# One core of a state-space mixer block: a smaller last transform, a new parameter table, and low weight parts kept in DRAM

## The chip, the core and the metric

The kernel runs on one core of a Trainium2 chip. The metric is the device time of one execution in microseconds (us), the median of several runs. A profiled execution gives a trace of every engine: PE (matrix multiply, with PEld for its weight loads), DVE (vector), ACT (activation functions and copies), POOL (general purpose, here mostly issuing transfers) and SP (issuing transfers only). Transfers issued by SP, ACT and POOL run on 16 shared DMA engines.

## The reference

With L = 2048 tokens and D = 576 channels, `_A_ref` is a state-space convolution along the tokens and `_B_ref` a two-layer network over the channels with F = 4608 hidden units:

```python
dt = jnp.exp(log_dt)
A = -jnp.exp(log_A_real) + 1j * A_imag
C = (C_real + 1j * C_imag) * dt[:, None]
P = jnp.exp((A * dt[:, None])[:, :, None] * pos[None, None, :])
K = 2.0 * jnp.einsum("dn,dnl->dl", C, P).real
y = irfft(rfft(u_t, 2 * L) * rfft(K, 2 * L))[:, :, :L]
s = y + u * D_skip
...
x = A_u
xn = _layernorm(x, axis=-1)
s = _A_ref(xn, ...)
g = _silu(_B_ref(xn, ...))      # layernorm, gelu(y @ w1 + b1) @ w2 + b2
return x + s * g
```

All data is 32-bit floating point.

## The kernel before

Two computations share the core.

**The network.** Tokens go in two halves of 1024, each half in two blocks of 512 (`tb`). The hidden units go in 12 groups of 384 (`g`). A slot is one group for one block, so there are 48 slots: 0 to 23 for the first half of the tokens, 24 to 47 for the second, and two neighbouring slots share a group's weights. To keep precision every operand is split into a high and a low part, and each product is three matmuls (high by high, low by high, high by low). In a slot, `layer1` (L511) makes three hidden tiles with 14 matmuls each, of which the ninth to twelfth and the last read the weights' low parts (`w1l`, `w1s`), and `layer2` (L568) makes eight pieces with 72 matmuls, every third of which reads `w2l`. `split_raw` makes the two parts: SP loads a piece of the weights into `raw` (L451 to L456), ACT rounds it to the high part (L491), DVE subtracts to get the low part (L488). Both halves of the tokens do this for the same 12 groups, so each weight is loaded and split twice. There is one buffer for each of `w1h`, `w1l`, `w2h`, `w2l`, so a group's parts are written after the last matmul of the group before has read its own: layer 1's while layer 2 of the odd slot runs, and layer 2's while layer 1 of the next slot runs.

**The convolution.** Channels go in six chunks of 96. Signal and kernel are cut into two halves of 1024 samples, and each is transformed in two steps. `forward` (L958) does 32-point transforms for both halves, a transpose on DVE (L945) follows, and `s2` (L996) does the 64-point step with the matrix `f2t`. DVE multiplies spectra: `prod` and `sums` (L1012 to L1020) form for the first output half x0 k0, and for the second x0 k1 + x1 k0, where the index names the half of the signal x and of the kernel k. `inverse` (L1042) does the 64-point step back with `g2t`, `back` (L1053) transposes, and `i1` (L1068) does the last 32-point step with `g1t`. In `i1` each matmul contracts over 128 rows, which are the real and imaginary parts of both halves, into 64 outputs: the second half of the output adds what runs over the end of the first half's linear convolution, taken from the imaginary parts with a sign (`odd_rows`). ACT copies the result out and POOL stores it with two transfers (L1077).

The convolution's kernel K itself is made on the chip. `params` computes for each channel and state its decay, angle, phase and size, and `pack` writes a table of 30 numbers for each of them: phase and angle, and powers of the decay with exponents 0 to 7, 0 to 24 in steps of 8 (also with 1024 added), 0 to 224 in steps of 32, and 0 to 768 in steps of 256. Each power is one ACT instruction over 144 channels (L764), the table goes to DRAM in four parts (L773). `tables` reads it back in 36 blocks of 16 channels (L786, on POOL), builds sines and magnitudes on ACT and DVE (L804 to L846), and `kgen` (L885) sums over the states on PE.

**The order.** Every engine's order is written by a planner, the class `Order`, which simulates the engines with estimated durations while it emits the instructions. Work of the network is placed first; steps of other lines (convolution, parameters, tables) are put in where an engine is estimated to be free. `pace` spreads the chunks over the kernel up to an estimated 1060 us. Each engine executes in this fixed order, and an instruction that waits holds up everything behind it on its engine. This holds also for transfers issued on POOL or SP. Towards the end the lines `combine` and `finish` form x + s g and store it.

Of the kernel before, what the change touches and what calls it, by code (L numbers as in the profile page):

```python
# [9 lines left out]
F32 = mybir.dt.float32  # L10
# [22 lines left out]
PK = 144  # L33
NXC, NROW = 1, 4
G = 3
# [18 lines left out]
class Order:  # L54
# [155 lines left out]
def mixer_kernel(ctx, tc, u, log_a_real, a_imag, c_real, c_imag, log_dt, d_skip, w1, b1, w2, b2,  # L210
# [40 lines left out]
    g1t = sb.tile([P, 2, 32], F32, name="g1t")  # L251
# [10 lines left out]
    def load_consts(g):  # L262
        r = slice(32 * g, 32 * g + 32)
        nc.gpsimd.dma_start(f1t[r], f1[r].rearrange("p (k m) -> p k m", k=8)[:, g::4, :])
        h, ri = divmod(g, 2)
        for k in range(h, 2):
            same = k == h
            part = ri if same else 1 - ri
            nc.gpsimd.dma_start(g1t[r, k], g1[64 * part:64 * part + 32, :32])
# [3 lines left out]
    def odd_rows():  # L273
        nc.vector.tensor_scalar(g1t[:32, 1], g1t[:32, 1], -1.0, None, op0=OP.mult)
# [28 lines left out]

    def scale_tv():
        nc.vector.tensor_scalar(tv[:, :32], tv[:, :32], -1.0, MID, op0=OP.mult, op1=OP.add)
        nc.vector.tensor_scalar(tv[:, 32:], tv[:, 32:], 32.0, MID, op0=OP.mult, op1=OP.add)
# [5 lines left out]
    nc.vector.memset(g1t[64:, 0], 0.0)  # L312
# [3 lines left out]
    acc = sb.tile([P, 8, D], F32, name="acc")  # L316


    A2 = sb.tile([P, 16, 2, CH, 2], F32, name="A2")
    A2F = A2.rearrange("p a b c r -> p (a b c r)")  # L320

    PT0 = 3 * D
# [22 lines left out]
    MV, SECOND, PAIR, M4 = {}, [], {}, []  # L345

    def norms(b0, n):
# [3 lines left out]
        def stats(t, part=None):  # L351
# [4 lines left out]
            elif t == 0:  # L356
                a, r = M4 if b0 == 4 else [sb.tile([P, 8], F32, name=m, bufs=2) for m in ("mv", "rs")]
# [107 lines left out]

    def split_raw(low_on=nc.vector):
# [4 lines left out]
        if which == 1:  # L471
            if i == 0 and k:
                w1_tiles()
# [7 lines left out]
        else:  # L481
            if i == 0:
                W[2] = (sb.tile([P, G, D], F32R, name="w2h"), sb.tile([P, G, D], F32R, name="w2l"))
# [3 lines left out]
        def low():  # L487
            low_on.tensor_sub(lo, r[:m], h[:m].bitcast(F32))  # L488
# [178 lines left out]
    def params():  # L667
# [8 lines left out]
        dt = sb.tile([P, 2, SB, 32], F32, name="U").rearrange("p a b c -> p (a b c)")[:, :D]  # L676
# [69 lines left out]
        early.append(step("DVE", d, lambda: V.tensor_mul(nrm, nrm, dt), need=["nrm"]))  # L746

        pt = A2F[:, PT0:PT0 + PK * NPAR].rearrange("p (d k) -> p d k", d=PK)
        ex = [(E1 + k, k) for k in range(1, 8)] + [(E8 + k, HALF * (k // 4) + 8 * (k % 4)) for k in range(1, 8)]
        ex += [(E32 + k, 32 * k) for k in range(1, 8)] + [(E256 + k, 256 * k) for k in range(1, 4)]  # L750

        def pack(i):
            s = slice(i * PK, (i + 1) * PK)

            def columns():
                if i == 0:
                    V.memset(pt[:, :, E1:E1 + 17:8], 1.0)
                V.tensor_copy(pt[:, :, 0], th[:, s])
                V.tensor_copy(pt[:, :, 1], ph[:, s])
                V.tensor_copy(pt[:, :, E256], cr[:, s])  # L760

            def powers(p):
                for k, m in ex[6 * p:6 * p + 6]:
                    A.activation(pt[:, :, k], nrm[:, s], AF.Exp, scale=-float(m))  # L764

            def rest():
                V.tensor_mul(pt[:, :, E256 + 1:], pt[:, :, E256 + 1:], bc(cr[:, s], 2, 3))
            for p in range(4):
                early.append(step("ACT", 1.85, lambda p=p: powers(p), tbl="exp", late=0.0,
                                  need=() if i else [("xn", b) for b in range(4, 8)]))  # L770
            early.append(step("DVE", 0.6 if i else 1.1, columns, need=["polar"]))
            early.append(step("DVE", 0.65, rest))
            early.append(step("POOL", 0.8, lambda: nc.gpsimd.dma_start(par_s[:, s, :], pt)))  # L773
            early.append(step(None, 8.0, lambda: None, mark=("pack", i)))
        for i in range(D // PK):
            pack(i)
        return out, early
# [17 lines left out]
    def tables(b):  # L795
# [36 lines left out]
        def weigh(k, part):  # L832

            if k == 0 and part == 0:
# [4 lines left out]
            if part == 0:  # L839
                nc.vector.tensor_mul(T["U"][:, k], w[:, k, :, 32:], m[:, :, 64:])  # L840
            elif part == 1:
                nc.vector.tensor_mul(v[:, k, :, :32], w[:, k, :, :32], m[:, :, :32])
            elif k == 0:
                nc.vector.tensor_mul(v[:, k, :, 32:], w[:, k, :, 31::-1], m[:, :, 32:64])
            else:
# [14 lines left out]
                + [step("DVE", dve(n), f(weigh, k, part), need=[("sin", b, k)] + ([("kg", b - 1)] if b else []),  # L860
                        mark=("wu", b, k) if part == 2 else None) for k in range(2) for part in range(3)])
# [53 lines left out]
    X1, S2, INV, I1, KG = 1.1, 1.75, 2.15, 3.05, 1.03  # L915

    def chunk(c):
# [24 lines left out]
        def spread(i, x):  # L942
            for g in range(4):
                c0 = 24 * g + 12 * i
                add("DVE", 0.65, lambda g=g, c0=c0: nc.vector.transpose(  # L945
# [20 lines left out]
        def k1(i):  # L966
# [7 lines left out]
            add("DVE", 0.2, skip, need=kt + ([("i1", c - 1)] if c else [("pack", D // PK - 1), ("mats", 3), "odd"] if i == 0 else []))  # L974
# [4 lines left out]
        def s2(p):  # L979
# [23 lines left out]
            def copy(i):  # L1003
                KK[i] = sb.tile([P, 2, 2, CH], F32, name="kk")
                nc.scalar.activation(KK[i], Q[i][:, :, 1::2], AF.Copy)

            def prod(i):

                if i == 0:
                    Y.append(ys_tile())  # L1010
                PR[i] = sb.tile([P, 2, 4 * CH], F32, name="pr").rearrange("p a (f d) -> p a f d", f=4)
# [497 lines left out]
```

## Time and profile before

| | |
|---|---|
| median of 3 runs | 1109.13 us (1109.07 to 1109.32) |
| profiled execution, its time | 1109.96 us |
| profiled execution, its span | 1107.5 us |
| granted PE clock | 0.998 |
| ACT busy | 670.0 us (60%) |
| POOL busy | 178.3 us (16%) |
| moved by DMA | 125.55 MB, 113 GB/s on average |

The span runs from the first to the last instruction. A row of a group gives the line of the code, the engine, the operation, the tile written and the tiles read, the shape, the number of instructions, the busy time in us and the mean of one in ns, then the engine's idle time just before them and what ended it. One matmul of plain 32-bit data leaves two records. "DMA landing" is the time from the issue of a transfer to its arrival.

### The profile page before, as it was taken

What the parts mean: (1) busy time and instruction counts of PE and PEld (TensorE: products, weight loads), DVE (VectorE), ACT (ScalarE), POOL (GpSimd) and SP (SyncE); (2) the same over time, 40 slices, a digit from 0 to 9 for tenths busy, and PEclk for the clock granted to TensorE, in tenths of its full rate; (3) what the DMA queues carried; (4) which work ended last, traced back from release to release, by engine and by line L of the source; (5) the groups of instructions that cost most, each with busy time, mean ns of one, the idle gap of its engine ahead of it and who ended that gap; (6) DMA issues with size and microseconds to landing.
All of it is one profiled execution on the core that took longest, in us unless ns stands there. A gap on an engine that the chain in (4) does not pass through costs nothing.

```text
span 1107.5 us, 27061 instructions
## 1 busy us (share of the span) xinstructions
PE 1087.3 (98%) x11451; PEld 944.0 (85%) x11451; DVE 917.3 (83%) x1508; ACT 670.0 (60%) x1012; POOL 178.3 (16%) x244
## 2 busy tenths in 40 slices
PE   8999999999999999999999999999999999999997
PEld 7988889879888888888888888888888888888896
DVE  7787566787799999998999988899899998676457
ACT  6586498867556674767856766566575655224333
POOL 5546423120000010000100000000010022010022
PEclk9999999999999999999999999999999999999999
DMA  7634545643224241244513422131422355353064
GB/s 235 228 127 151 169 149 186 202 125 120 63 65 120 35 124 43 75 125 88 182 38 107 84 70 79 46 106 47 100 80 65 104 120 177 100 157 96 17 206 125
DMA packets 110041, 125.55 MB, mean 113 GB/s; under 512 B 59364, under 2 KB 80688, under 8 KB 109408
## 3 DMA queue, kind: packets, MB, share of 16 engines
q1 hardware_dynamic: 95728, 76.44, 24.6%
q0 software_dynamic: 13632, 46.49, 13.3%
q8 instruction: 90, 1.47, 0.5%
q10 hardware_dynamic: 560, 0.89, 0.3%
q14 instruction: 31, 0.25, 0.1%
HBM read 95.53 MB, written 34.01 MB: 117 GB/s over the span
## 4 chain that ended last, share of the span: by engine, by line
PE 86%; DVE 6%; ACT 4%; DMA 2%; issue 1%; SPq 0%; DVEq 0%; ACTq 0%
PE mxb L568 19%; PE mxa L568 19%; PE mxa L511 18%; PE mxb L511 18%; PE cv L885 3%; PE cv L996 3%; PE cv L958 2%; PE cv L1068 2%; PE cv L1042 1%; DMA raw<-in_B_w_dram 1%; DMA xc<-xn_s 1%; PE cv L416 1%; DVE acc L576 1%; ACT h L544 1%; DVE hl L550 0%
## 5 line engine op out<-in xcount | busy, mean ns | idle before, releaser
L550 DVE TENSOR_TENSOR hl<-h,hh 128x512 fp32r<-128x512 f32 x144 | 98.6, 687 | 95.9 <-ACT hh L547 95.2
L568 PE MATMUL mxa<-w2h,hh 128*128 128x288 f32 x573 | 171.6, 299 | 1.0 <-DVE acc L576 0.9
L568 PE MATMUL mxb<-w2h,hl 128*128 128x288 f32 x576 | 170.3, 296 | 1.6 <-DVE hl L550 1.6
L568 PE MATMUL mxb<-w2h,hh 128*128 128x288 f32 x576 | 171.8, 298 | 0.1
L568 PE MATMUL mxa<-w2h,hl 128*128 128x288 f32 x573 | 169.7, 296 | 1.0 <-DVE hl L550 0.8
L568 PE MATMUL mxb<-w2l,hh 128*128 128x288 f32 x576 | 169.9, 295 | 0.0
L568 PE MATMUL mxa<-w2l,hh 128*128 128x288 f32 x573 | 169.0, 295 | 0.0
L544 ACT ACTIVATE h<-mxa,b1t 128x512 f32<-128x512 f32 x73 | 50.1, 687 | 138.3 <-PE mxa L511 136.6
L786 POOL DMA_DIRECT2D par<-par_s x36 | 27.4, 761 | 571.3 <-DVE mg L829 528.9
L568 PEld LDWEIGHTS mxa<-w2h,hh 128*128 128x128 f32 x573 | 107.8, 188 | 9.2 <-issue 4.9
L568 PEld LDWEIGHTS mxb<-w2h,hh 128*128 128x128 f32 x576 | 108.4, 188 | 7.5 <-issue 1.5
L568 PEld LDWEIGHTS mxb<-w2h,hl 128*128 128x128 f32 x576 | 108.3, 188 | 1.8 <-DVE hl L550 1.8
L568 PEld LDWEIGHTS mxa<-w2h,hl 128*128 128x128 f32 x573 | 107.7, 188 | 1.7 <-DVE hl L550 1.7
L568 PEld LDWEIGHTS mxb<-w2l,hh 128*128 128x128 f32 x576 | 108.4, 188 | 0.7
L568 PEld LDWEIGHTS mxa<-w2l,hh 128*128 128x128 f32 x573 | 107.8, 188 | 0.7
L547 ACT ACTIVATE hh<-h 128x512 fp32r<-128x512 f32 x144 | 90.5, 630 | 3.6
L544 ACT ACTIVATE h<-mxb,b1t 128x512 f32<-128x512 f32 x71 | 48.8, 688 | 72.4 <-PE mxb L511 71.6
L491 ACT ACTIVATE w2h<-raw 128x576 fp32r<-128x576 f32 x72 | 44.9, 676 | 70.3 <-PE mxa L568 64.5
L576 DVE TENSOR_TENSOR acc<-mxa,acc 128x576 f32<-128x576 f32 x88 | 65.8, 748 | 17.4 <-PE mxa L568 17.3
L511 PE MATMUL mxb<-XH,w1h 128*128 128x512 f32 x280 | 78.2, 401 | 1.9 <-ACT h L544 1.9
L511 PE MATMUL mxa<-XH,w1h 128*128 128x512 f32 x284 | 79.2, 401 | 0.0
L576 DVE TENSOR_TENSOR acc<-mxb,acc 128x576 f32<-128x576 f32 x88 | 66.2, 752 | 15.2 <-PE mxb L568 14.8
(236 smaller groups left out, 2455.3 us busy)
## 6 DMA issues: line engine op xcount, KB each, us to landing
raw<-in_B_w_dram SPq DMA_DIRECT2D x72, 288.0 KB, 3.1
raw<-in_B_w_dram SPq DMA_DIRECT2D x96, 192.0 KB, 3.0
par_s<-A POOLq DMA_DIRECT2D x4, 2160.0 KB, 8.1
par<-par_s POOLq DMA_DIRECT2D x36, 240.0 KB, 3.4
f2t<-f2q SPq DMA_DIRECT2D x24, 256.0 KB, 3.7
raw<-in_B_w_dram SPq DMA_DIRECT2D x48, 96.0 KB, 3.8
xc<-xn_s SPq DMA_DIRECT2D x48, 96.0 KB, 4.0
u_s<-in_A_u_dram POOLq DMA_DIRECT2D x16, 288.0 KB, 4.5
```

What stands on the lines that cost most here:

```text
L491: nc.scalar.activation(h, r, AF.Copy)
L511: nc.tensor.matmul(q, a, b, start=j == 0, stop=j == len(ops) - 1)
L544: nc.scalar.activation(t, q, AF.Gelu_apprx_tanh, bias=b1t[:, g * G + i:g * G + i + 1], scale=1.0)
L547: LAST[0] = nc.scalar.activation(hh[:, i], t, AF.Copy)
L550: nc.vector.tensor_sub(hl[:, i], t, hh[:, i].bitcast(F32))
L568: nc.tensor.matmul(q[:, dh, :288], a[:, i, c], b[:, i, d], start=i == 0 and k == 0, stop=i == G - 1 and k == 2)
L576: nc.vector.tensor_add(o, q[:, dh:dh + n, :288], b if g == 0 else o)
L786: nc.gpsimd.dma_start(PAR[b].rearrange("p (g i) k -> p g (i k)", g=4), dram(par_s, (b // 6 * CH + b % 6 * 4) * NPAR, [[D * NPAR, P], [24 * ...
L885: nc.tensor.matmul(q[32 * g:32 * g + 32, i // 2, i % 2 * 64:i % 2 * 64 + 64], U[:, ri, 4 * g + i, :], v[:, ri, 4 * g + i, :], start=ri == ...
L958: nc.tensor.matmul(Q1ST[i, x][g // 2][64 * f:64 * f + 64, g % 2].rearrange(order), f1t[r].rearrange("p s k -> p (s k)"), rhs(r, f), start= ...
L996: nc.tensor.matmul(Q[i][32 * q:32 * q + 32, f, 2 * ri:2 * ri + 2], m[r, 4 * i + q, 32 * ri:32 * ri + 32], A2[r, 4 * p + 2 * i + q // 2, :, ...
L1068: nc.tensor.matmul(Q[h][64 * y:64 * y + 64, t], g1t.rearrange("p f a -> p (f a)"), A2[:, k:k + 2, 1].rearrange("p i d r -> p i r d"), star ...
```

## The change

It has five parts. (1) The last transform uses only the real parts of each half: `g1t` becomes a 64-row, 32-column matrix (used for each half by itself), and `i1` issues 16 matmuls of 64 rows and 32 outputs in place of 8 of 128 rows and 64 outputs. What runs over from the first half is put into the kernel's spectrum: `cross` adds a turned k0 to k1 before the product. The result lies differently on the partitions, so it is stored with eight transfers per chunk in place of two. (2) The parameter table is made in eight parts of 72 channels with two buffers. A DVE multiplication makes all 28 exponents' arguments at once, and one ACT instruction the exponentials of half a part. (3) In the first half of the tokens POOL stores the low parts of each group's weights to DRAM after the split. In the second half POOL loads them back; DVE doesn't subtract there, and the rest of the split (load of `raw`, high part on ACT) stays. (4) In `weigh` the two multiplications for sine and cosine become one of double length. (5) Small items: statistics of the norms lie in the tile `U`, conditions of some steps are changed, the planner counts the load of an activation table as possible while it waits, and several of its estimated durations are new.

```diff
     def take(self, eng, dur, ready, tbl=None):
-        start = max(self.t[eng], ready)
+        free = self.t[eng]
         if tbl and tbl != self.tbl:
-            dur += 1.28
+            free += 1.28
             self.tbl = tbl
+        start = max(free, ready)
...
-PK = 144
+NEXP = NPAR - 2
+PK = 72
...
+    def lows_on(g, which, back):
+
+        pairs = ([(W[1][1], lo1_s[g]), (w1s[:64], lor_s[g])] if which == 1 else [(W[2][1], lo2_s[g])])
+        for a, b in pairs:
+            nc.gpsimd.dma_start(a if back else b, b if back else a)
...
         def low():
-            low_on.tensor_sub(lo, r[:m], h[:m].bitcast(F32))
+            if half == 0:
+                low_on.tensor_sub(lo, r[:m], h[:m].bitcast(F32))
             for _ in range(NEXT[which - 1][i]):
                 load_raw()
...
+            def scaled(p):
+                e = slice(p * h, (p + 1) * h)
+                V.tensor_mul(pt[:, e, 2:], bc(nrm[:, i * PK + p * h:i * PK + (p + 1) * h], 2, NEXP), bc(expo, 1, h))
+
+            def powers(p):
+                e = slice(p * h, (p + 1) * h)
+                A.activation(pt[:, e, 2:], pt[:, e, 2:], AF.Exp, scale=-1.0)
             def columns():
-                if i == 0:
-                    V.memset(pt[:, :, E1:E1 + 17:8], 1.0)
                 V.tensor_copy(pt[:, :, 0], th[:, s])
                 V.tensor_copy(pt[:, :, 1], ph[:, s])
-                V.tensor_copy(pt[:, :, E256], cr[:, s])
-
-            def powers(p):
-                for k, m in ex[6 * p:6 * p + 6]:
-                    A.activation(pt[:, :, k], nrm[:, s], AF.Exp, scale=-float(m))
-
-            def rest():
-                V.tensor_mul(pt[:, :, E256 + 1:], pt[:, :, E256 + 1:], bc(cr[:, s], 2, 3))
+                V.tensor_mul(pt[:, :, E256:], pt[:, :, E256:], bc(cr[:, s], 2, 4))
...
             if part == 0:
-                nc.vector.tensor_mul(T["U"][:, k], w[:, k, :, 32:], m[:, :, 64:])
+                nc.vector.tensor_mul(T["U"], w[:, :, :, 32:], bc(m[:, :, 64:], 1, 2))
             elif part == 1:
-                nc.vector.tensor_mul(v[:, k, :, :32], w[:, k, :, :32], m[:, :, :32])
+                nc.vector.tensor_mul(v[:, :, :, :32], w[:, :, :, :32], bc(m[:, :, :32], 1, 2))
...
-    X1, S2, INV, I1, KG = 1.1, 1.75, 2.15, 3.05, 1.03
+    X1, S2, INV, I1, KG = 1.05, 1.7, 1.95, 1.75, 1.06
...
             def copy(i):
-                KK[i] = sb.tile([P, 2, 2, CH], F32, name="kk")
-                nc.scalar.activation(KK[i], Q[i][:, :, 1::2], AF.Copy)
+                KK[i] = sb.tile([P, 5, CH], F32, name="kk")
+                nc.scalar.activation(KK[i][:, 0:2], Q[i][:, 0, 1::2], AF.Copy)
+                nc.scalar.activation(KK[i][:, 4], Q[i][:, 0, 1], AF.Copy, scale=-1.0)
+            def cross(i):
+                nc.vector.tensor_add(KK[i][:, 2:4], Q[i][:, 1, 1::2], KK[i][:, 1::3])
+                nc.vector.tensor_mul(Y[0][:, i], bc(Q[i][:, 1, 0::2], 2, 2), bc(KK[i][:, 0:2], 1, 2))
...
-                for h in range(2):
-                    for t in range(2):
-                        for y in range(2):
-                            k = 8 * y + 4 * h + 2 * t
-                            nc.tensor.matmul(Q[h][64 * y:64 * y + 64, t], g1t.rearrange("p f a -> p (f a)"),
-                                             A2[:, k:k + 2, 1].rearrange("p i d r -> p i r d"),
+                for t in range(2):
+                    for e in range(4):
+                        for f in range(2):
+                            r = slice(64 * f, 64 * f + 64)
+                            k = 4 * e + 2 * t
+                            nc.tensor.matmul(Q[f][32 * e:32 * e + 32, t], g1t[r],
+                                             A2[r, k:k + 2, 1].rearrange("p i d r -> p i r d"),
                                              start=True, stop=True, skip_group_check=True)
...
-                nc.gpsimd.dma_start(s_s[:, 8 * h:8 * h + 8, c * CH:(c + 1) * CH], sc.rearrange("p t i d -> p (t i) d"))
+                for e in range(4):
+                    y, h = divmod(e, 2)
+                    nc.gpsimd.dma_start(s_s[64 * y + 32 * f:64 * y + 32 * f + 32, 8 * h:8 * h + 8, c * CH:(c + 1) * CH],
+                                        sc[32 * e:32 * e + 32].rearrange("p t i d -> p (t i) d"))
...
+        if half == 0:
+            lw["steps"].append(step("POOL", 1.7 if which == 1 else 0.9, lambda: lows_on(g, which, False), need=[("w", k)]))
+        else:
+            (w1_tiles if which == 1 else w2_tiles)()
+            lw["steps"].append(step("POOL", 1.7 if which == 1 else 0.9, lambda: lows_on(g, which, True)))
+            lw["steps"].append(step(None, 6.0, lambda: None))
+            for j in range(k - m + 1, k + 1):
+                lw["steps"].append(step(None, 0.0, lambda: None, need=[("wl", j)], mark=("w", j)))
...
-        gl["steps"].append(step("POOL", 2.2, lambda g=g: load_consts(g), need=[("xn", NT - 1)]))
+        gl["steps"].append(step("POOL", 2.2, lambda g=g: load_consts(g), need=[("xn", 11)]))
```

The line `lw` stands first among the planner's lines. In `weigh_in` the loads back are emitted right after the matmul block that reads the old parts last, and the planner counts the parts as ready 6 us after the issue.

More of the change, by code (lines that the diff above doesn't have):

```diff
@@ L481, in split_raw @@
         else:
-            if i == 0:
-                W[2] = (sb.tile([P, G, D], F32R, name="w2h"), sb.tile([P, G, D], F32R, name="w2l"))
+            if i == 0 and half == 0:
+                w2_tiles()
             h, lo = W[2]
@@ L768, in pack @@
[L768 to L774, printed above, removed]
+                V.tensor_mul(pt[:, :, E256:], pt[:, :, E256:], bc(cr[:, s], 2, 4))
@@ new lines, in pack @@
+            for p in range(2):
+                need = (["nrm2", "expo"] + [("xn", b) for b in range(4, 8)]) if i == 0 else [("pack", i - 2)] if i > 1 else ()
+                product.append(step("DVE", 1.25, lambda p=p: scaled(p), need=() if p else need, mark=("scaled", i, p)))
+                power.append(step("ACT", 1.2, lambda p=p: powers(p), tbl="exp", late=0.0, need=[("scaled", i, p)]))
+            power[-1]["mark"] = ("power", i)
+            early.append(step("DVE", 0.85, columns, need=["polar", ("power", i)]))
```

117 lines of the change are left out of this document (65 added, 52 removed).

## The prediction

> **What bounds the kernel now.** I read the page first: busy shares, slices and the chain that ended last.
>
> ```profile
> span 1107.5 us, 27061 instructions
> PE 1087.3 (98%) x11451; PEld 944.0 (85%) x11451; DVE 917.3 (83%) x1508; ACT 670.0 (60%) x1012; POOL 178.3 (16%) x244
> PE   8999999999999999999999999999999999999997
> PE 86%; DVE 6%; ACT 4%; DMA 2%; issue 1%; SPq 0%; DVEq 0%; ACTq 0%
> ```
>
> PE is busy 98% of the span and carries 86% of the chain; no slice between the first and the last falls below nine tenths. Next come the stretch that holds the second half's slots, and PE's own waits.
>
> ```profile
> 530.00:1100.00 570.00, 567.93 (x6497) 488.44 (x6496) 479.82 (x784) 311.61 (x449) 60.75 (x96) 1.00 0.35 98
> ...
> PE cv L1042 <- issue: 2.2, 1, 2.2
> PE mxb L511 <- ACT h L544: 1.9, 2, 1.5
> PE cv L416 <- DVE rs L1153: 1.8, 1, 1.8
> PE cv L958 <- DVE kt L970: 1.7, 1, 1.7
> PE mxb L568 <- DVE hl L550: 1.6, 1, 1.6
> ...
> PE mxa L568 <- DVE acc L576: 0.9, 2, 0.6
> PE mxa L568 <- DVE hl L550: 0.8, 2, 0.6
> ```
>
> The first row gives window, length, then busy time of PE, PEld, DVE, ACT and POOL. In the second half PE lacks 2.1 us of 570, and DVE has 90 us free. So DVE time is not what sets the end: all PE waits for DVE in these rows sum to 1.8 + 1.7 + 1.6 + 0.9 + 0.8 = 6.8 us in the whole kernel. The time is the sum of PE's work, plus some ten us of waits, plus an ending. A change counts if it removes PE work or makes PE wait.
>
> **The change part by part.** Part 1, the last transform, is the only one that removes PE work. PE's timeline shows a last transform between two network blocks, then a `forward`; and elsewhere an `s2`.
>
> ```profile
> 404.22 0.39 PE L511 MATMUL mxa<-XR,w1s 128*128 128x512 f32 x1
> 404.54 2.92 PE L1068 MATMUL cv<-A,g1t 128*64 128x384 f32 x16
> 407.39 1.20 PE L511 MATMUL mxb<-XH,w1h 128*128 128x512 f32 x4
> ...
> 410.79 0.90 PE L958 MATMUL cv<-kt,f1t 32*64 32x384 f32 x16
> ...
> 317.16 0.30 PE L568 MATMUL mxb<-w2h,hl 128*128 128x288 f32 x1
> 317.39 1.60 PE L996 MATMUL cv<-A,f2t 64*32 64x192 f32 x64
> ```
>
> Two records are one matmul. The last transform is 8 matmuls of 384 columns, each on a 128 x 64 piece of the array, so two fit beside each other and four follow one another: 2.92 us. The new one is 16 matmuls of 384 columns on pieces of 64 x 32, the shape of `s2`. `s2` has 32 matmuls of 192 columns on that shape, the same sum of columns (6144) over the same eight pieces, the two halves alternating in the same way: 1.60 us. So I take 2.92 - 1.60 = 1.32 us for each chunk, six chunks: -7.9 us. Bounds: two runs of `forward`, which does 8 matmuls of 384 columns on eight pieces in 0.90 us, would be 1.80 us, so -6.7 us; two matmuls deep in place of four, half of 2.92 or 1.46 us, -8.8 us. [...]
>
> The spectrum pays for part 1 on DVE and ACT. `cross` adds 48 DVE instructions of 192 elements, and one ACT copy of 384 elements becomes two of 192 and 96.
>
> ```profile
> L1019 DVE TENSOR_TENSOR ys<-pr 128x192 f32<-128x192 f32 x48 | 17.2, 358 | 1.7
> L1005 ACT ACTIVATE kk<-cv 128x384 f32<-128x384 f32 x48 | 23.0, 480 | 18.1 <-DVE ys L1014 15.7 <-DVE ys L1020 2.2
> L890 ACT ACTIVATE kt<-cv 128x256 f32<-128x256 f32 x36 | 13.3, 371 | 17.2 <-PE cv L958 10.8 <-PE cv L1042 2.6 <-PE cv L1068 2.5
> ```
>
> DVE: 48 x 0.358 = +17 us. ACT: between 0 and 48 x (2 x 0.371 - 0.480) = +12.6 us. PE doesn't wait for a spectrum (no such row above), and does network work meanwhile, so I take 0.
>
> The store with eight transfers per chunk lengthens POOL's issue from 2 x 0.90 to 8 x 0.55 us or so (rows of L1077 and L605 in the last fence of this part): +2.6 us of POOL per chunk, up to 8 x 0.90 - 1.80 = +5.4. Behind them wait table loads and the low parts' loads.
>
> Parts 2 and 4 change DVE and ACT alone.
>
> ```profile
> 72.06 5.30 ACT L764 ACTIVATE A<-A 128x144 f32<-128x144 f32 x18
> L816 ACT ACTIVATE w<-w 128x1024 f32<-128x1024 f32 x36 | 38.0, 1056 | 23.3 <-DVE w L813 23.1
> L829 DVE TENSOR_TENSOR mg<-par 128x1024 f32<-128x1024 f32 x36 | 44.0, 1221 | 0.6
> L842 DVE TENSOR_TENSOR v<-w,mg 128x512 f32<-128x512 f32 x72 | 49.3, 684 | 0.0
> 80.00:200.00 120.00, 117.56 (x755) 106.08 (x754) 79.62 (x126) 87.49 (x165) 50.17 (x73) 1.00 0.47 152
> ```
>
> The 96 powers take 96 x 5.30 / 18 = 28 us of ACT; 16 exponentials over 36 x 28 = 1008 elements take 16 x 1.056 = 17 us: -11 us. DVE gets 16 multiplications of that size, 16 x 1.221 = +20 us, and has 120 - 80 = 40 us free between 80 and 200 us, where the table is made. In `weigh` two instructions of 0.684 become one of 1.221, twice in each of 36 blocks: -10.6 us of DVE. None of it is on PE: 0. Without that room the table, and with it the first chunk, would come up to 20 us later; PE would do network work first, and the chunks have room before the end.
>
> Part 3 relieves DVE in the second half and adds transfers.
>
> ```profile
> L488 DVE TENSOR_TENSOR w2l<-raw,w2h 128x576 fp32r<-128x576 f32 x72 | 51.8, 755 | 17.5 <-ACT w2h L491 17.5
> L488 DVE TENSOR_TENSOR w1l<-raw,w1h 128x384 fp32r<-128x384 f32 x94 | 47.9, 558 | 0.0
> L488 DVE TENSOR_TENSOR w1s<-raw,w1r 64x384 fp32r<-64x384 f32 x23 | 12.5, 542 | 0.0
> raw<-in_B_w_dram SPq DMA_DIRECT2D x72, 288.0 KB, 3.1
> par_s<-A POOLq DMA_DIRECT2D x4, 2160.0 KB, 8.1
> L773 POOL DMA_DIRECT2D par_s<-A x4: 584/592/600, 115.1 to 198.9; - x4
> 1062.11 3.19 PE mxb L511 x14
> ...
> 1071.65 1.58 PE mxa L568 x12
> ...
> 1081.17 0.92 PE mxa L511 x4
> 1049.02 0.94 POOL L1077 DMA_DIRECT2D s_s<-pr  x1 [50.53 <-ACT pr L1076]
> 884.88 0.55 POOL L605 DMA_DIRECT2D row<-u_s  x1
> ```
>
> DVE loses half of these: 51.8/2 + 47.9 x 48/94 + 12.5 x 12/23 = -57 us, all in the stretch where PE lacks 2.1 us; the gain in time is between 0 and 2.1, and I take 0. Now the loads. A group's `w2l` is 3 x 288 = 864 KB, and `w1l` with `w1s` 4 x 192 + 96 = 864 KB too. Between the rows of 288 KB (3.1 us) and 2160 KB (8.1 us) 864 KB lands in 3.1 + 5.0 x 576/1872 = 4.6 us; from above, three loads of 288 KB one after the other, 9.3 us. With one issue of 0.59 us `w2l` is there 5.2 us (at most 9.9) after layer 2 ends, and layer 1, which covers it, takes 1071.65 - 1062.11 = 9.5 us. `w1l` and `w1s`, two issues, are there after 5.8 us (at most 10.5); layer 2 covers 1081.17 - 1071.65 = 9.5 us, and eight matmuls of the next layer 1 come before the first that reads `w1l`, 8 x 3.19/14 = 1.8 us. So 0 is taken; the upper end costs 0.4 us for each of 12 groups, +5 us. The stores of the first half (36 issues of 0.59 us, 21 us of POOL) have two slots to finish: 0.
>
> Where the load waits for PE's last matmul, table loads, spectrum stores and the ending's transfers wait behind it on POOL. It is emitted when that matmul is, so the wait is one matmul block, about 3 us, and the table loads are a whole block of 16 channels ahead: 0.
>
> Part 5 and the order: new conditions and estimates reorder every engine. Waits that depend on the order (2.2 + 1.7 + 1.6 + 0.8 in PE's rows) can go, -6.3 us, or as many again can come, +6.3 us. I take 0, as the new order is made by the same planner with the same room before each deadline.
>
> The sum is -7.9 us on a profiled time of 1109.96, so 1102.1 us; that execution lies 0.83 us above the median of the runs, so the forecast for the median is 1109.13 - 7.9 = **1101.2 us**. With the ends it runs from -8.8 - 6.3 (1094) to -6.7 + 6.3 (1109).
>
> **The rivals.** First, the relieved DVE and earlier raw loads also clear the order's waits: -7.9 - 6.3, 1095 us (1109.13 - 14.2 = 1094.9). For it: the longest wait for `hl` begins with a late load of raw weights.
>
> ```profile
> 771.91 7.86 SPq L928 DMA_DIRECT2D xc<-xn_s  x8
> 779.87 3.86 DMA raw<-in_B_w_dram
> ```
>
> Against it: that load was late because SP was held 7.9 us by a chunk's signal load (`xc`), which stays.
>
> Second, slower: the low parts come too late. The place is the first matmul that reads `w2l` in each group of the second half, and the mechanism POOL's fixed order: the load's issue stands behind output transfers that wait for DVE, and its data shares the DMA engines with the raw loads. It decides from 9.5 us after layer 2's end. With the upper landing of 9.3 us, the issue of 0.59 and two stores of 0.9 ahead of it, it comes after 11.7 us: 2.2 us late, 12 times, +26 us less 7.9, 1127 us. It becomes a loss from 0.7 us late each time. Against it: the first matmuls are covered by twice the likely landing, and the DMA engines are busy only 35% in that stretch (0.35, the last figure but one of its row).
>
> Third, no change: transfers stretch the signal loads, and SP's raw loads behind `xc` come later still. 864 KB take 5.0 x 864/1872 = 2.3 us of the engines; a stall of that size in each of the four chunks of the second half is 9 us, 1110 us. For it: the two rows above, one stall of 1.6 us at the end of them. Against it: the row of that wait counts one, for six signal loads. [...]
>
> Fourth, the change doesn't do what it says: the pieces of the two halves don't run beside each other. Then only four pieces work at once, 16 matmuls are four deep as before, 2.92 us stay, and the time is 1109 us. `s2` on the same shape speaks against it.
>
> **How the numbers follow.** Forecast 0.66, first rival 0.13, second 0.10, third 0.07, fourth 0.04. A measurement of this kernel tells 0.2%, 2.2 us, from no change. Faster: 0.66 + 0.13 and 0.01 of the third's milder form, 0.80. Same: the fourth and most of the third, 0.09. Slower: 0.11 with what is left of the third. The range leaves out the second rival and part of the fourth and third, and spans the ends of the sum: 1095 to 1108.5 us.
>
> **What would show it.** Right: L1068's successor with 32 records in 1.6 us for each chunk; PE busy some 8 us less; DVE some 30 us less busy in all; the loads of `w1l` and `w2l` landing in 4 to 6 us and no PE wait that a DMA or POOL ends. Wrong: PE waits of 1 us or more in front of the matmuls that read `w2l`, at every second slot; new waits in the slots after an `xc` load; or a last transform above 2 us.

## The result, and the profile after

The changed kernel takes 1140.77 us (median of 4 runs, 1137.86 to 1142.24) against 1109.1 us before on the same chip, a ratio of 1.028 (95% interval 1.0254 to 1.0302): slower by 32 us, where 7.9 us less was forecast. The page of the changed kernel (profiled execution: 1137.86 us):

```profile
span 1136.1 us, 27207 instructions
PE 1100.6 (97%) x11547; PEld 950.1 (84%) x11547; DVE 894.8 (79%) x1414; ACT 649.2 (57%) x973; POOL 237.9 (21%) x354
PEclk9999989999999999999899999999999989999999
PE 74%; DVE 7%; DMA 7%; issue 5%; POOL 5%; ACT 1%; SPq 0%; DVEq 0%; POOLq 0%; ACTq 0%
```

PE has work of 1100.6 us where it had 1087.3, although its last transforms became shorter; its share of the chain fell from 86 to 74%; and three slices of the granted clock are below nine tenths. The rows that the prediction named as tests, from the costliest groups and the DMA issues (count, KB of each, us from issue to landing):

```profile
L1093 PE MATMUL cv<-A,g1t 64*32 64x384 f32 x192 | 9.6, 504 | 0.0
raw<-in_B_w_dram SPq DMA_DIRECT2D x72, 288.0 KB, 4.6
lo_s<-w2l POOLq DMA_DIRECT2D x12, 864.0 KB, 5.6
w2l<-lo_s POOLq DMA_DIRECT2D x12, 864.0 KB, 4.9
w1l<-lo_s POOLq DMA_DIRECT2D x12, 768.0 KB, 5.3
```

The last transform takes 9.6 / 6 = 1.60 us, as forecast, and the low parts land in 4.9 and 5.3 us. The price is elsewhere. PE's waits (line, what for: us in total, times, longest):

```profile
PE mxa L582 <- DVE acc L590: 13.4, 4, 4.6
PE cv L1066 <- issue: 5.7, 4, 2.1
PE mxa L582 <- DVE hl L564: 3.4, 7, 1.3
PE mxb L525 <- DMA w1l<-lo_s: 1.4, 1, 1.4
```

A low part is waited for once. The long waits are for `acc`, the addition out of PSUM on DVE, near 155, 558 and 930 us, and for nothing that the profile shows ("issue"), in the inverse transform. The chain through the second of the long ones (start, us, what):

```profile
546.24 0.40 issue
546.64 0.11 POOL w1l L477
546.75 0.46 issue
547.21 0.54 POOL w1s L477
547.75 7.79 DMA par<-par_s
...
555.63 1.24 DVE w L820
...
556.89 0.69 DVE w L823
557.59 0.68 DVE acc L590
...
558.31 3.73 PE mxa L582 x14
```

A load of table parameters (`par`) is issued on POOL behind the spectrum's stores and two loads of low parts; it takes 7.79 us, DVE stands at the table's first instruction, and the addition that frees PE's bank is behind it in DVE's fixed order. Then the same work of PE takes twice its time. Windows of that stretch (busy us of PE, PEld, DVE, ACT, POOL; then granted clock, DMA share, GB/s):

```profile
553.50:556.30 2.80, 0.38 (x3) 0.14 (x2) 0.67 (x1) 0.00 (x0) 0.00 (x0) 1.00 0.14 42
556.30:563.10 6.80, 4.79 (x19) 4.79 (x20) 6.56 (x12) 3.91 (x9) 1.17 (x3) 0.50 0.13 46
563.10:569.90 6.80, 6.80 (x32) 5.48 (x32) 6.54 (x11) 6.69 (x11) 2.28 (x4) 1.00 0.92 291
```

The clock is 0.50 for 6.8 us. This begins 2.0 us before PE goes on at 558.31, so 4.8 us of PE's work fall into it and half of that is lost: a matmul of layer 2 takes 3.73 / 14 = 0.27 us, where the prediction's row of before has 1.58 / 12 = 0.13 us. The wait near 930 us has another load ahead of it: there the loads of the ending's rows stand on POOL behind a chunk's eight stores, and DVE waits for a row that takes 4.72 us to land. The last difference is small and everywhere. Blocks of layer 1 on the chains of waits of before, and of after:

```profile
1065.31 3.17 PE mxa L511 x14
1068.48 3.17 PE mxb L511 x14
```

```profile
1009.32 3.26 PE mxa L525 x14
1012.58 3.25 PE mxb L525 x14
```

Start to start, the median of layer 1's matmuls is 227 ns before and 232 ns after, with the same operands, shapes and clock. There are 48 slots of 42 such matmuls: 2016 x 5 ns = 10 us by the median, and 8.4 us by the sum over all of them.

These terms make up the loss. From the start of PE's first matmul to that of its last, the changed kernel's trace is 28.7 us longer than that of before. Waits are 15.5 us more, half clock costs 9.5 us, layer 1's pace 8.4 us, and the last transform gives back 7.9 us; some 3 us are spread over the other steps.

### The profile page after: what moved, and what is told of

Same layout as the page of the kernel before. It is cut to its first block, busy times and chain, and to the rows that moved or that the text cites. A ratio compares the mean times of both kernels' runs of the same rounds, so it can differ in the third digit from the quotient of the medians.

```text
span 1136.1 us, 27207 instructions
## 1 busy us (share of the span) xinstructions
PE 1100.6 (97%) x11547; PEld 950.1 (84%) x11547; DVE 894.8 (79%) x1414; ACT 649.2 (57%) x973; POOL 237.9 (21%) x354
## 4 chain that ended last, share of the span: by engine, by line
PE 74%; DVE 7%; DMA 7%; issue 5%; POOL 5%; ACT 1%; SPq 0%; DVEq 0%; POOLq 0%; ACTq 0%
PE mxa L582 16%; PE mxb L582 16%; PE mxa L525 16%; PE mxb L525 15%; PE cv L902 3%; PE cv L1013 3%; PE cv L1066 2%; DMA raw<-in_B_w_dram 2%; DMA par<-par_s 1%; PE cv L975 1%; DMA par_s<-A 1%; POOL s_s L1104 1%; DMA row<-g_s 1%; DVE w L820 1%; DMA w1l<-lo_s 1%
## 5 line engine op out<-in xcount | busy, mean ns | idle before, releaser
L582 PE MATMUL mxa<-w2h,hh 128*128 128x288 f32 x573 | 174.2, 304 | 13.4 <-DVE acc L590 13.4
L582 PE MATMUL mxa<-w2h,hl 128*128 128x288 f32 x573 | 172.8, 301 | 3.4 <-DVE hl L564 3.4
L582 PE MATMUL mxa<-w2l,hh 128*128 128x288 f32 x573 | 171.4, 299 | 0.0
L582 PEld LDWEIGHTS mxa<-w2h,hh 128*128 128x128 f32 x573 | 110.2, 192 | 21.2 <-DVE acc L590 14.6
L582 PEld LDWEIGHTS mxa<-w2h,hl 128*128 128x128 f32 x573 | 110.3, 192 | 5.2 <-DVE hl L564 5.2
L582 PEld LDWEIGHTS mxa<-w2l,hh 128*128 128x128 f32 x573 | 110.4, 193 | 0.7
```

Of the source, the lines that this page charges most:

```text
L582: nc.tensor.matmul(q[:, dh, :288], a[:, i, c], b[:, i, d], start=i == 0 and k == 0, stop=i == G - 1 and k == 2)
```

## The experiments

**The parts of the change, alone and left out.** `nolow` leaves part 3 out: the low parts are subtracted on DVE in both halves, and nothing of them is moved.

```
-            if half == 0:
-                low_on.tensor_sub(lo, r[:m], h[:m].bitcast(F32))
+            low_on.tensor_sub(lo, r[:m], h[:m].bitcast(F32))
...
-            lw["steps"].append(step("POOL", 1.7 if which == 1 else 0.9, lambda: lows_on(g, which, True)))
```

> The changed kernel without part 3: no transfer of low parts, DVE subtracts in both halves. Theory A (the low parts' transfers on POOL's queue make table loads and other loads late, DVE waits for them in its fixed order, and the accumulation behind it keeps PE waiting): the waits of PE for acc at 155 and 558 us (4.6 and 4.4 us) go with the half clock after each of them, the one at 930 us (behind the eight stores of a chunk) stays; about 15 to 18 us less than the changed kernel, 1122 to 1126 us. Theory B (the new order by the new estimates makes the waits itself): PE's waits stay at 25 us or more and the time within 5 us of the changed kernel, 1136 to 1146 us. The layer 1 block of 14 matmuls is some 3.25 us in the changed kernel and 3.18 before: if that comes with the part 3 transfers, it is 3.18 here.

Measured 1107.25 us, ratio 0.9966 (0.9952 to 0.998). The long waits and the half clock are gone; layer 1 stays at 232 ns. This is 15 us below what theory A expected, as the wait near 930 us went too, and the waits for nothing that shows fell from 5.7 to 2.0 us.

`p1only` is the kernel before with part 1 alone (last transform and spectrum).

> The kernel before with part 1 alone (last transform, spectrum, eight stores per chunk, and the estimates of these steps; the norms' statistics lie in a free part of A2 for room). By the prediction's main term, 6 x 1.32 us of PE go: 1101 us, between 1096 and 1106 with the waits of a new order. Theory B' (any new order costs waits of ten us or more): 1111 us or more. The eight stores on POOL can delay the ending's loads: then a wait of PE near 930 us of 3 to 4 us with a half clock after it, and 1107 us. Layer 1 blocks: 3.18 us as before if the longer block of the changed kernel comes from its transfers or its memory layout, 3.25 if it comes from the chip or from part 1.

Measured 1130.66 us, ratio 1.0178 (1.0163 to 1.0193). Layer 1 is at 235 ns, 11 us more by the sum over all its matmuls, and PE's last matmul starts at 1098 us, 31 us ahead of the end: the last chunk's last transform comes at 1074 us (1046 before), and the ending has only begun. PE's waits are fewer than before (7.5 us against 12.6 in its rows of waits), so the time is as theory B' had it, but the cause is not.

`lowsp` is the changed kernel with the low parts on SP's queue, counted there by the planner.

```
-            nc.gpsimd.dma_start(a if back else b, b if back else a)
+            a, b = a.bitcast(F32), b.bitcast(F32)
+            nc.sync.dma_start(a if back else b, b if back else a)
...
-            lw["steps"].append(step("POOL", 1.7 if which == 1 else 0.9, lambda: lows_on(g, which, True)))
+            lw["steps"].append(step("SP", 1.7 if which == 1 else 0.9, lambda: lows_on(g, which, True)))
```

> The changed kernel with the low parts' transfers issued on SP's queue in place of POOL's (the same bytes at about the same time). Theory A1 (it is POOL's order that makes the table loads late): the waits at 155 and 558 us go, about 1122 to 1126 us, unless SP's own loads become late. Theory A2 (it is the bytes, which share the 16 DMA engines): table loads still land in 6 to 8 us next to the low parts, and the time stays within 5 us of the changed kernel.

Measured 1118.44 us, ratio 1.0067 (1.0043 to 1.009); no wait is longer than 2.6 us. So part 3 carries most of the loss, but the order was made anew in both kernels. Two runs keep every order as it is. `nodma` leaves out the low parts' transfers alone (the second half multiplies by the last group's low parts), `sameorder_sp` issues them on SP, with the diff of `lowsp` but not its planner's line.

> The changed kernel with every engine's order kept, and the low parts' transfers left out: no stores in the first half, no loads in the second, where layer 1 and layer 2 read the low parts of the last group instead (that part of the result is left out). It prices the transfers by themselves. Theory A (they make other loads late, and that stalls DVE and with it PE): no wait of PE for acc above 1 us, no half clock before the end, 1110 to 1116 us. Theory B (the order makes the waits): within 5 us of the changed kernel.

> The changed kernel with every order kept but that the low parts' transfers are issued on SP in place of POOL; the planner still counts them on POOL, so nothing else moves. Theory A1 (POOL's fixed order): the waits at 155, 558 and 930 us fall below 2 us, 1115 to 1122 us. Theory A2 (the bytes on the DMA engines): table loads next to low parts still land in 6 to 8 us, the waits stay, 1133 us or more.

`nodma` took 1123.34 us, ratio 1.0122 (1.0109 to 1.0135): without the transfers 17.4 us are gone, but 14 us more than before on its chip (1109.66 us) remain, outside both expectations, and with them stalls at the same places. Its waits and its chain at 155 us:

```profile
PE mxa L584 <- DVE acc L592: 8.8, 5, 3.8
PE cv L1068 <- issue: 4.5, 3, 1.7
...
140.94 8.51 DMA par_s<-A
...
149.74 0.46 POOL f2t L283
...
150.27 3.23 DMA par<-par_s
...
153.62 1.22 DVE w L822
154.84 0.68 DVE acc L592
```

The table load stands on POOL behind a load of constants (`f2t`) whose last issue waits for the store of the table. No low part is near. `sameorder_sp` took 1134.93 us, ratio 1.0223 (1.0203 to 1.0243): the stalls stay (`acc` 11.0 us), as theory A2 expected, so POOL's queue alone is not the cause either.

**Where the tiles lie.** `moved` is the changed kernel with two small tiles (`dsk`, `st`, 640 bytes a partition) allocated ahead of `XH` and not behind it. `align` is a loop of layer-1 matmuls on zeros and nothing else, at 16 x 16 offsets of the two operands in steps of 32 bytes. `layout` makes `moved`'s edit in the kernel before:

```
-    dsk = sb.tile([P, D // 4], F32, name="dsk")
...
+    dsk = sb.tile([P, D // 4], F32, name="dsk")
+    MV["st"] = sb.tile([P, 2, 6], F32, name="st")
     XH = sb.tile([P, KB, 2, TB], F32R, name="XH")
```

> The changed kernel with two small tiles laid before XH, XL and XR, so that these lie 640 bytes further on, as in the kernel before when taken modulo 512; no instruction changes its place. If the place in memory sets the longer layer 1 block (some 3.25 us against 3.18 before), the blocks shorten to 3.18 us and the time falls by 48 x 3 x 0.07 = 10 us to 1130 us; if it doesn't, nothing changes, 1138 to 1143 us.

> Not the computation: 256 blocks of 14 matmuls shaped as in layer 1 on zeros, one block for each of 16 places of the moving operand and 16 places of the weights, in steps of 32 bytes over 512; all else is left out and zeros go to the output. If the place of the moving operand sets the pace, blocks differ by line (each line is one place of the moving operand, over all places of the weights): about 227 ns a matmul at some places and 232 to 235 at others. If it is the distance between the two operands, all lines have the same mean and the blocks within a line differ. If neither, all blocks take the same time.

> The kernel before with nothing changed but the place of two small tiles (dsk and st, 640 bytes a partition, now ahead of XH instead of behind it). XH minus w1h goes from 0 to 128 modulo 256 bytes, the value of the kernel after the change. Theory (placement sets layer 1's pace): matmuls of layer 1 start 232 ns apart instead of 227, 48 blocks of 42 give 2016 x 5 ns, +10 us, 1119 us; PE's waits stay as they are. Rival (the wider pitch came from traffic or from the order): 227 ns and 1109 us.

`moved` took 1135.81 us, ratio 1.0229 (1.0199 to 1.0259): layer 1 is back at 227 ns, but only 5 of the 10 us are gained. Summed over all its matmuls, layer 1 takes 5.1 us less, where the pace alone would give 8.4, and PE's waits grow by 2.4 us. `layout` took 1119.14 us, ratio 1.0078 (1.0057 to 1.0098): layer 1 of an otherwise unchanged kernel goes from 227 to 232 ns, +8.5 us. Its blocks on the chain of waits:

```profile
1048.38 3.26 PE mxa L512 x14
1051.64 3.26 PE mxb L512 x14
```

In `align` all 16 lines are equally long (54.6 us) and the blocks within a line differ, so it is the distance between the operands that counts. The median of start to start:

```
moving operand's address minus the weights', modulo 256 bytes    ns
0                                                                227
64                                                               229
32, 96, 128, 160, 192, 224                                       232 to 234
```

The kernels agree to 2 ns, by the difference `XH` - `w1h`: 0 in the kernel before and `moved` (227), 128 after and in `layout` (232), 192 in `p1only` (235). The change keeps the norms' statistics in the tile `U`, and so drops the tiles `mv` and `rs`, four of 32 bytes, that lay between `XH` and `w1h`: these are 128 bytes nearer to each other than before.

`best` is `nolow` with `moved`'s edit.

> The changed kernel without part 3, with the operands XH, XL and XR 640 bytes further on as in the run 'moved'. The run without part 3 took 1107 us with layer 1 blocks of 3.25 us; with blocks of 3.18 us 144 x 0.07 = 10 us less, 1097 us, 1094 to 1100: faster than both kernels. If the place matters only beside other traffic, 1105 us or more.

Measured 1103.6 us, ratio 0.9946 (0.9935 to 0.9958): 0.5% faster than before, but above the expected 1094 to 1100 us. Against `nolow`, layer 1 takes 6.4 us less by its sum, not 10, and PE's waits grow by 1.1 us. `lowsp_moved` is `lowsp` with that edit.

> The kernel after with the low parts' transfers on SP's queue, counted there by the planner (lowsp, 1118.4 us), and the two small tiles ahead of XH (as in moved). Theory (the two causes add): layer 1 at 227 ns instead of 232 takes 10 us off lowsp, 1108 us, no PE wait over 3 us. Rival (they don't add, since in moved the pace alone gave back only 5 us): 1113 us or more, with the gained time turned into waits.

Measured 1115.52 us, ratio 1.005 (1.0033 to 1.0067): layer 1 runs at 227 ns, but only 3 of 10 us arrive: by its sum it takes 6.0 us less, and PE's waits grow by 3.6 us. The causes do not add; the rival was right.

**The stalls for `acc`.** `parsp` keeps the order of `moved` and issues the table loads on SP; `parplan` leaves them on POOL and corrects the planner's estimate.

```
-            nc.gpsimd.dma_start(PAR[b].rearrange("p (g i) k -> p g (i k)", g=4), dram(
+            nc.sync.dma_start(PAR[b].rearrange("p (g i) k -> p g (i k)", g=4), dram(
```

```
-        return ([step(None, 3.0, lambda: load_par(b), mark=("par", b), need=[("pack", ((b // 6 + 1) * CH - 1) // PK)]
+        return ([step("POOL", 0.8, lambda: load_par(b), need=[("pack", ((b // 6 + 1) * CH - 1) // PK)]
                       + ([("mags", b - 2)] if b > 1 else [("xn", k) for k in range(8, NT)])),
+                 step(None, 7.0, lambda: None, mark=("par", b)),
```

> The kernel moved (after, two small tiles ahead of XH, 1135.8 us) with every order kept, but the loads of the table's parameters (par) issued on SP's queue instead of POOL's. Theory (the stalls near 155 and 558 us are table loads that stand behind constant loads and spectrum stores on POOL): both stalls shrink to under 1 us and the half clock behind them goes, each 2 to 2.5 us of wait and 3.4 us of clock, so 10 to 12 us less, 1124 to 1126 us; the one near 930 us, behind the ending's row loads, stays. Rival (the load is late by its own time beside other transfers, wherever it is issued, or SP's order holds up the raw weights instead): 1133 us or more, with waits for hl or for w1h in place of acc.

> The kernel moved (1135.8 us) with the planner told what the traces show of a table load: an issue of 0.8 us on POOL and 7 us until the data is there, in place of 3 us on no engine. The load keeps its queue. Theory (the stalls come from that estimate): DVE's work is ordered for a later table and no longer stands in front of the PSUM additions, waits for acc fall from 13.5 to under 4 us, 1120 us or less. Rival (the transfers' traffic and POOL's queue decide, not the estimate): waits of more than 10 us for acc or for rows stay, 1130 us or more.

`parsp` took 1134.45 us, ratio 1.0215 (1.0188 to 1.0242). The stall near 558 us is gone. That near 155 us stays: the load is issued at 144.01 us, 5.5 us earlier than in `moved`, but it takes 9.10 us, beside the table's store (141.15 to 150.35 us).

```profile
144.01 9.10 DMA par<-par_s
```

New waits for low parts (4.0 us) and for `acc` come later. The rival was right for this stall, and for the time. `parplan` took 1119.25 us, ratio 1.0071 (1.0049 to 1.0093), 16.6 us less than `moved`, with all transfers on their queues. DVE's waits for `par` and for the ending's rows, in `moved`, then in `parplan`:

```profile
DVE w L821 <- DMA par<-par_s: 14.5, 3, 6.0
DVE row L628 <- DMA row<-g_s: 9.6, 3, 4.7
```

```profile
DVE row L628 <- DMA row<-g_s: 6.4, 2, 5.1
```

The load takes no less time (median 4.2 us from issue to landing), but no table instruction stands on DVE ahead of its data, and PE's waits for `acc` fall from 13.5 to 1.2 us. So the stalls came from the planner's 3.0 us on no engine for a load that needs an issue on a crowded queue and up to 7.8 us. The estimate alone does not make them: before and `nolow` have it too, with loads of up to 6.9 us, and no such stall. It takes an order in which part 3's transfers are placed as well.

**The waits in the inverse.** What `parplan` has left is "issue", 8.0 us in four waits at L1068. Its chain at one of them:

```profile
500.63 1.03 PE cv L904 x64
501.66 1.73 PE cv L1068 x95
503.39 2.67 issue
506.05 0.38 PE cv L1068 x3
506.43 3.84 PE mxa L526 x9
```

A table transform of 64 records stands directly ahead of the inverse, which stops three matmul records before its end (the chain's row counts 95 of the 125 ahead of the stop). Among the DMA packets of the changed kernel's trace there are 90 of 16 KB on a queue named instruction, one for 257 of PE's 23094 matmuls and weight loads. Beside the stalls (us):

```
kernel    inverse stops   goes on    instruction packet    packet's end to going on
before         506.77     509.21      506.61 to 507.77      1.44
after          375.38     377.36      375.12 to 376.08      1.28
after          667.16     669.49      666.74 to 667.87      1.62
after          785.89     787.27      784.77 to 785.94      1.33
best           645.90     647.47      645.05 to 646.07      1.40
parplan        370.54     372.33      370.11 to 371.07      1.26
parplan        503.14     506.05      502.74 to 504.56      1.49
parplan        643.39     646.08      643.83 to 644.82      1.26
parplan        878.55     880.08      877.84 to 878.78      1.30
```

All nine have the table transform directly ahead, and each goes on 1.3 to 1.6 us after a packet's end. Shorter stops also come without that pair, as at 901.44 us in the changed kernel or right behind an inverse. In the traces of all 15 kernels 43 of the 44 waits of over 0.3 us that are put down to issue end 1.3 to 1.6 us after such a packet. That PE runs out of instructions there, with 192 records and as many weight loads in 3.1 us (1.03 + 1.73 + 0.38 in the chain above), is an estimate from these times; no row shows it. `spaced` (from `parplan`) and `best_spaced` (from `best`) forbid that pair in PE's order.

```
+                inverse = (h[0]["mark"] or ("",))[0] == "inv"
+                if x is kl and dense:
+                    break
+                dense = dense or inverse
-                behind = ride(h[0]) if x in (c1, c3) else None
+                behind = ride(h[0]) if x in (c1, c3) and not inverse else None
```

> The kernel parplan (1119.3 us) with one more rule for PE's order: a block of the table's transform (64 records) is not put directly ahead of an inverse transform (128 records), nor behind it. In parplan that stands six times, and in four of them the inverse stops for 1.5 to 2.9 us in its middle. Theory (there PE runs out of instructions: 192 matmul records and as many weight loads come in 3.2 us, and each of these stalls ends 1.3 to 1.5 us after a 16 KB packet of the instruction queue ended): without the pair the waits called issue fall from 10.3 us to under 3, and with them four half clocks of 3.4 us; 8 us of waits and 4 x 1.7 us of clock less, 1104 to 1108 us. Rival (the inverse waits for a late load of its matrices, g2t, behind the low parts): the waits stay in front of or in the inverse, 1115 us or more.

> The kernel best (after without part 3, two small tiles ahead of XH; 1103.6 us) with the same rule: the table's transform is not put next to an inverse. In best the pair stands five times, two of them stall for 1.6 and 0.6 us. Theory (instructions run out there): issue waits fall from 1.7 us to under 0.5, 1100.5 to 1103 us. Rival (other order effects of one to three us decide): between 1102 and 1107 us.

`spaced` took 1107.26 us, ratio 0.9969 (0.9959 to 0.9979): 12.0 us less than `parplan`, and faster than before, with every part of the change in. Its waits:

```profile
PE mxa L583 <- DVE acc L591: 2.4, 2, 1.3
PE mxa L583 <- DVE hl L565: 2.2, 5, 0.8
PE mxa L583 <- DMA w2l<-lo_s: 1.8, 1, 1.8
...
PE mxb L583 <- issue: 0.9, 1, 0.9
```

No inverse waits any more, with the same transfers, and the matrices of the four that stopped in `parplan` had landed 25 us or more ahead: that these came late is ruled out. Three of those four stops were followed by a half clock, not all four as expected. The 0.9 us that are left stand right behind an inverse and end 1.45 us after a packet, so the rule takes away the long stops, not what the stops have in common. `best_spaced` was a miss, 1125.66 us, ratio 1.0134 (1.0113 to 1.0154), above both expectations. Its end, by windows:

```profile
1100.00:1102.50 2.50, 0.38 (x3) 0.15 (x2) 1.50 (x3) 0.68 (x1) 0.00 (x0) 1.00 0.62 219
1102.50:1124.20 21.70, 0.00 (x0) 0.00 (x0) 9.94 (x17) 2.14 (x4) 7.46 (x13) 0.55 0.52 145
```

PE is done at 1100 us, and 24 us of combining and storing follow. The rule moved the last chunk's last transform from 1035 to 1073 us, as in `p1only` (1074); in the kernels where it starts by 1058 us the end follows PE's last matmul by 8 us. Nothing was gained ahead of that either: PE's last matmul starts 6.5 us later than in `best`, and the waits put down to issue rose from 1.7 to 4.0 us. One of them, 2.3 us at the 64-point step, ends 14 us after the last packet; its cause stays open.

## Why the prediction was wrong

**Part 1** held: 1.60 us for each chunk, -7.9 us. The 64 x 32 pieces run beside each other (eight records start within 0.05 us, the next eight 0.36 us after the first), so the fourth rival with its 2.92 us is out.

**The spectrum, parts 2 and 4** were taken as 0, and DVE is busy 22.5 us less in all (894.8 against 917.3; forecast 30). No PE wait of the rows above ends at the spectrum. But these instructions were not varied by themselves.

**Part 3** is where the forecast fails first. Its own test was passed: 4.9 and 5.3 us of landing against 4.6, and one wait of 1.4 us for a low part. So the second, slower rival, low parts that come too late, is not what happened, though its sign was right. The sentence that failed is the next one: "the table loads are a whole block of 16 channels ahead: 0". They are not. A load is emitted when a buffer comes free, and the planner then counts on it after 3.0 us. The median of its landing is 3.4 us, but behind eight stores and two low parts on POOL it took 7.8, and near 155 us a constant load that waits held up its issue. The raw loads are longer too (4.6 against 3.1 us). In the order of the changed kernel the transfers cost 17.4 us (`nodma`), though PE waits only 1.4 us for a low part itself. In an order planned with a longer time for the load, the kernel with part 3 is 1107.3 - 1103.6 = 3.7 us behind the fastest one without it (`spaced` against `best`, from two chips; the ratios differ by 0.23%). As the orders differ too, this is no clean price of part 3.

**Part 5 and the order** got 0, with 6.3 us either way. PE's waits grew by 15.5 us instead, which rules out the first rival too. Two things made that bound too small. It was the sum of the order's waits of before, and PE's clock was left out: each of the three longest waits (4.6, 4.4 and 3.6 us) comes with 6.8 us at clock 0.50. PE works in 4.8 to 5.5 us of these and loses half, 2.4 to 2.7 us. And the pair of table transform and inverse, which happens to stall once before (the row of 2.2 us in the prediction, taken there for a wait of the order), stalls three times after and four times in `parplan`. Correcting the load's estimate and then forbidding the pair takes 16.6 + 12.0 us off `moved`.

**The statistics in the tile `U`**, a small item of part 5, were not priced at all. With them the tiles `mv` and `rs` go, and `XH` lies otherwise to the weights: 8.5 us by `layout`.

The sum that the runs give: from 1140.8 us, 5.0 for the place, 16.6 for the table loads' estimate and 12.0 for the pair lead to 1107.3 us. The forecast of 1101.2 us is reached by none; `best`, the nearest, is 0.54% below before, 6.0 us of the 7.9. What holds `spaced` another 3.7 us behind `best` was not separated: the low parts' wait of 1.8 us and other orders are in it.

**The third rival**, raw loads stretched by the low parts, has half its mechanism in the rows (3.1 to 4.6 us), but waits for `hl` total 3.4 us, not the 9 it asked for.

## What to carry to other kernels

Before pricing a change as hidden, look at which estimate the order was made with: a load that the planner expected after 3.0 us and that took 7.8 held up DVE here, and PE behind it for 4.4 us. A stall can be paid again in clock: those of 4.6, 4.4 and 3.6 us came with 6.8 us at clock 0.50 each, one of 1.7 us with 3.4 us, and one of 2.1 us with none. Compare the addresses of PE's operands when a tile is allocated elsewhere, and the start-to-start time of a matmul that the diff doesn't touch; a uniform 2% (227 to 232 ns) is not a wait and stands in no row of waits. Look at the places where a run of small matmuls stands unbroken ahead of another (four stops of the inverse, 8.0 us, in `parplan`, none in `spaced`), and check when the last dependent block starts, not only when PE ends.

## What the hardware showed

The start-to-start time of a 128x512 matmul went with where its operands lie to each other. In `align`, on zeros, it was 227 ns at 0 bytes modulo 256, 229 ns at 64, and 232 to 234 ns at the other multiples of 32; the kernels show 227 ns at 0, 232 ns at 128 and 235 ns at 192, and in `layout` the place alone took it from 227 to 232 ns.

In the changed kernel the half clock began at fixed steps of time: its stretches begin at 153.53, 378.81, 556.30, 928.36 and 1133.16 us, which lie 66, 52, 109 and 60 steps of 3.41 us apart, and the first four last 6.83, 3.41, 6.83 and 6.83 us. It went with how long PE is busy within one step. With the traces of before and after cut at such steps, those at full clock with 1.68 us of PE's work or less were followed by half clock (after: 0.21, 1.68, 0.99, 1.31 and 0 us ahead of the five stretches; before: 1.48 us ahead of the one that begins at 1102.16 us), and none with 1.81 us or more was. In `parplan` a step with 1.86 us was followed by it, and in `sameorder_sp` one with 1.65 us was not, so that between these two both occur. So 1.8 us between two matmuls' starts were enough in `parplan`, where they lie in one step (the first two rows), and 3.3 us from 927.33 us on were not in `sameorder_sp`, where they lie in two (the last three). The rows are windows of one step each, PE's busy time first, with the granted clock third from the end:

```profile
370.13:373.54 3.41, 1.86 (x98) 1.56 (x89) 3.41 (x5) 1.36 (x3) 0.75 (x1) 1.00 0.05 14
373.54:376.95 3.41, 3.41 (x16) 3.41 (x16) 0.77 (x1) 3.39 (x5) 0.00 (x0) 0.50 0.27 72
925.49:928.90 3.41, 2.13 (x17) 1.90 (x15) 0.11 (x1) 0.00 (x0) 0.00 (x0) 1.00 0.55 210
928.90:932.31 3.41, 1.65 (x12) 1.65 (x13) 2.34 (x4) 0.00 (x0) 2.07 (x4) 1.00 0.25 54
932.31:935.72 3.41, 3.41 (x36) 2.65 (x35) 2.24 (x5) 0.00 (x0) 0.65 (x2) 1.00 0.60 182
```

At the nine places of the table above, where a table transform stands directly ahead of an inverse, PE stopped for 1.4 to 2.9 us, and each time went on 1.26 to 1.62 us after the end of a 16 KB packet on the instruction queue. The two are 192 matmul records and as many weight loads, 3.1 us of work in the chain of `parplan`. Why PE stops at one such place and not at another was not settled.
